# Block-sparse attention feeding soft mixture-of-experts slots: score groups, weight loads, slot steps and output halves in another order

## The chip, the cores and the metric

The kernel runs on one core of a Trainium2 chip. The metric is the device time of one execution in microseconds (us). Three executions were timed. A separate execution was recorded by the hardware profiler; all durations quoted from a profile belong to that one.

## The reference

q, k and v have the shape 4 x 8 x 768 x 64 (batch, head, position, width). First comes attention that keeps six chunks of 32 keys for each query:

```python
k_min, k_max = min/max of k over each chunk of 32 keys
ub = sum(maximum(q * k_min, q * k_max))        # an upper bound of the score, per query and chunk
top_chunks = argsort(where(causal, ub, -1e9))[..., -6:]
scores = where(sel & causal, q @ k.T / 8, -1e9)
x = softmax(scores) @ v                        # laid out as 3072 x 512
```

Its result goes through a soft mixture of 8 experts with 4 slots each:

```python
logits = x @ phi                               # 3072 x 32
d = softmax(logits over the 3072 rows)         # dispatch
slot_input = d.T @ x                           # 32 x 512
slot_out[e] = relu(slot_input[e] @ w1[e]) @ w2[e]      # 512 -> 1024 -> 512, per expert
out = softmax(logits over the 32 slots) @ slot_out     # combine, 3072 x 512
```

The inputs are float32 in HBM; the kernel loads them as bf16. Eight w1 and eight w2, each 2 MB in HBM and 1 MB as bf16, make 16 weights, called w_sb 0 to 15.

## The kernel before, in words

The work is cut into 16 pairs of heads; four pairs make a batch. A loop of steps, `for i in range(-2, NPAIR)` at L479, runs a software pipeline that is written out by hand: each engine runs its instructions in the order in which the step function calls stand there. In step i these pairs are at work:

- Pair i + 4: its k and q are loaded (`load`, L129). Pair i + 2: its v is loaded (`load_v`, L134); its k and q are transposed on TensorE and copied out by ScalarE (`transposes` L181, `evac_T` L190), and VectorE takes the chunks' minima and maxima (`kmin`, `kmax`) and splits q by sign (`qsplit`).
- Pair i + 1: upper bounds on TensorE (`ubound`), the six best chunks on VectorE (`select`: twelve MAX8 at L241 and a comparison at L244), and transposition of the selection (`ns_transposes`, `evac_ns`).
- Pair i: scores and exponentials. The 21 causal blocks of 128 x 128 are packed into six groups of 384 or 512 columns (table `GROUPS`). `scores(i, g)` makes one matmul for q and k (L270) and one or two for the mask (L280) for each piece of a group and head, into one of two PSUM buffers `sc`; `expo(i, g)` runs one exponential on ScalarE (L293) and masks the diagonal block on GpSimd (L295).
- Pair i - 1: product with v (`pv`, L314), in four portions. Pair i - 2: normalisation on VectorE (`normalise`, L326 and L327) and transposition of the result (`x_transposes`, `evac_x`).

When the last pair of a batch has come to step i - 3, the step is a slot step (steps 6, 10 and 14): the batch's logits get their running column maximum (`moe_max`: a transpose on TensorE; `moe_bound`: a maximum on VectorE, L379; `moe_exp`: broadcast matmul at L385 and subtraction on GpSimd; `moe_exp2`), the row maximum and exponentials of the combine weights (`moe_comb`, `moe_comb2`), the accumulation of the slot inputs (`moe_dispatch`, L439) and the transposed combine weights (`moe_ct`, L453 and L456). Logits are formed at the end of the step before (`moe_logits`). Small PSUM results share two rotating buffers `tp`.

All loads, the weights included, are issued on GpSimd's queue (L122, L129, L134), between that engine's masks and small operations. The table `wplan` (L468) says how many weights each step issues: weight 0 ahead of the loop, then one in step -1 and in each of the steps 2 to 15. Up to step 13 they are issued in the middle of the step, behind the v load; in steps 14 and 15, where space has come free, at the top.

Behind the loop comes the tail (from L568): the last pair's attention, the last batch's logits, maxima, dispatch and combine weights, with a few matmuls that do nothing but keep TensorE running (`keep`, L584). Then the experts: first layer (`experts_in`, L670; two halves f of the hidden width), transposition (`hidden_T`, L682), second layer (`experts_out`, L710; hidden half f, expert group g of four experts, output column half y), scaling by the slots' sums (`zsum`, L690; so_sb at L729 and L731) and the sums of the combine weights (`csums`, 24 matmuls at L697). Last, 24 row blocks of the output: two matmuls of 256 columns each (L749), a scaling by VectorE or ScalarE (L752 to L756) and a store on SP's queue (L759, L761), mostly of 512 KB.

Of the kernel before, what the change touches and what calls it, by code (L numbers as in the profile page):

```python
# [30 lines left out]
    [(0, 0, 384, 0)],  # L31
    [(1, 0, 256, 0), (0, 384, 128, 256)],
    [(2, 0, 512, 0)],
    [(5, 0, 128, 0), (1, 256, 384, 128)],
    [(3, 0, 384, 0)],
    [(4, 0, 256, 0), (0, 512, 256, 256)],
]
WIDTH = [sum(p[2] for p in g) for g in GROUPS]
BLOCK = {}
for _g, _pieces in enumerate(GROUPS):  # L40
    for _kg, _q0, _w, _c in _pieces:
        for _x in range(0, _w, P):
            BLOCK[(_kg, _kg + (_q0 + _x) // P)] = (_g, _c + _x)


@with_exitstack
def kernel(
# [41 lines left out]
    w_sb = []  # L89
    for i in range(EARLY):  # L90
        w_sb.append(static.tile([P, NDG * F], BF16, name=f"w_sb{i}"))
# [171 lines left out]
    def scores(i, g):  # L263
        ps = p_sc.tile([P, 2, 512], F32, name="sc_ps", tag="sc")
        kT, qT, nsT = st["kT", i], st["qT", i], st["nsT", i]
        for kg, q0, w, c in GROUPS[g]:
# [20 lines left out]
    def expo(i, g):  # L287
        w = WIDTH[g]
        if w == 512:
            e = ep.tile([P, 2, 512], BF16, name="e_sb", tag="e_sb")  # L290
        else:
            e = ep3.tile([P, 2, 384], BF16, name="e3_sb", tag="e3_sb")
        nc.scalar.activation(e[:, :, :w], st.pop(("scps", i, g))[:, :, :w], func=ACT.Exp, scale=scale)  # L293

        nc.gpsimd.affine_select(  # L295
            out=e[:, :, :P], in_=e[:, :, :P], compare_op=ALU.is_ge, fill=0.0,
            base=0, pattern=[[0, 2], [1, P]], channel_multiplier=-1,
        )
        st["e", i, g] = e

    def pv(i, ts):
# [7 lines left out]
        for t in ts:  # L309
            for h in range(2):  # L310
                o = at[:, h, (t - tb) * (D + 1):(t - tb + 1) * (D + 1)]
                for kg in range(t + 1):
                    g, c = BLOCK[(kg, t)]
# [68 lines left out]
    def moe_exp(b):  # L382
        lg = st["lg", b]
# [32 lines left out]
    def moe_comb(b):  # L416

        lg = st.pop(("lg", b))
# [31 lines left out]
    def moe_ct(b):  # L450
# [5 lines left out]
        nc.vector.tensor_copy(cT_all[:, b * NQT:(b + 1) * NQT, :], ps)  # L456
# [11 lines left out]
    wplan = {i: 1 for i in range(-1, NPAIR)}  # L468
    for i in (0, 1):
        wplan[i] = 0  # L470
# [8 lines left out]
    for i in range(-2, NPAIR):  # L479
# [4 lines left out]
        if have(i):  # L484
            scores(i, 0)
            expo(i, 0)
            scores(i, 1)
            expo(i, 1)
        moe(moe_max, i - 3)
        if have(i + 1):  # L490
            ubound(i + 1)
        if have(i - 2):
            normalise(i - 2)
        moe(moe_bound, i - 3)
        if have(i + 1):
            select(i + 1)
        if i == -1:
# [13 lines left out]
        moe(moe_exp, i - 3)  # L511
# [5 lines left out]
        moe(moe_exp2, i - 3)  # L517
# [4 lines left out]
        if have(i + 2):  # L522
            transposes(i + 2, "q")
            evac_T(i + 2, "q")
            kmin(i + 2)
        if have(i - 2):
# [4 lines left out]
        moe(moe_comb, i - 3)  # L531
# [4 lines left out]
        if have(i):  # L536
            scores(i, 4)
            expo(i, 4)
            if i == LAST:
                pv(i - 1, [5])  # L540
            scores(i, 5)
            expo(i, 5)
        moe(moe_comb2, i - 3)
# [68 lines left out]
    keep(2)  # L612
# [12 lines left out]
    nc.vector.tensor_reduce(rm, lg1, axis=AX.X, op=ALU.max)  # L625
    dm = small.tile([P, 1, NS], F32, name="dm", tag="dm")
# [13 lines left out]
    op = ctx.enter_context(tc.tile_pool(name="op", bufs=5))  # L640
# [17 lines left out]
    cinv = tail.tile([P, B * NQT], F32, name="cinv")  # L658
    zinv = tail.tile([P, 1], F32, name="zinv")
# [28 lines left out]
    def zsum():  # L688
        ps = p_tp.tile([P, 1], F32, name="z_ps", tag="tp")
        nc.tensor.matmul(  # L690
            ps, lhsT=zrow.rearrange("p j s -> p (j s)"), rhs=identf[:1, :1], start=True, stop=True)
        nc.vector.reciprocal(zinv, ps)

    def csums():
        ps = p_tp.tile([P, B * NQT], F32, name="cs_ps", tag="tp")
        for n in range(B * NQT):
            nc.tensor.matmul(  # L697
                ps[:, n:n + 1], lhsT=cT[:, n // 2, n % 2], rhs=ones_sq[:, :1], start=True, stop=True)
        nc.vector.reciprocal(cinv, ps)

    HD = Dm // 2
    so_t = p_at.tile([P, 2, 512], F32, name="so_ps", tag="at")
    so_ps = [so_t[:, y, :HD] for y in range(2)]
# [20 lines left out]
    experts_out(0, [0], [0, 1])  # L724
    hidden_T(1)
    zsum()
    experts_out(0, [1], [0, 1])
    experts_out(1, [0, 1], [0])
    nc.scalar.activation(so_sb[0], so_ps[0], func=ACT.Copy, scale=zinv)  # L729
    experts_out(1, [0, 1], [1])  # L730
    nc.scalar.activation(so_sb[1], so_ps[1], func=ACT.Copy, scale=zinv)  # L731
    csums()


    homes = ((p_sc, "sc"), (p_tp, "tp"), (p_sc, "sc"), (p_tp, "tp"), (p_at, "at"))
    n = 0
    for m in range(B * NQT // 2):
        o_sb = op.tile([P, 2, Dm], F32, name="o_sb", tag="o_sb")
        rows = out[m * 2 * P:(m + 1) * 2 * P, :].rearrange("(p x) d -> p x d", x=2)
        for x in range(2):  # L740
            pool, tag = homes[n % 5]
            if n == 0:
                o_ps = pool.tile([P, 2, Dm], F32, name="o2_ps", tag=tag)
                halves = [o_ps[:, y, :HD] for y in range(2)]
            else:
                o_ps = pool.tile([P, Dm], F32, name="o_ps", tag=tag)
                halves = [o_ps[:, y * HD:(y + 1) * HD] for y in range(2)]
            for y in range(2):
                nc.tensor.matmul(halves[y], lhsT=cT[:, m, x], rhs=so_sb[y], start=True, stop=True)  # L749
            if n == 0:  # L750
                for y in range(2):
                    nc.vector.tensor_scalar_mul(o_sb[:, x, y * HD:(y + 1) * HD], halves[y], cinv[:, n:n + 1])  # L752
            elif x == 0:
                nc.vector.tensor_scalar_mul(o_sb[:, x, :], o_ps, cinv[:, n:n + 1])
            else:
                nc.scalar.activation(o_sb[:, x, :], o_ps, func=ACT.Copy, scale=cinv[:, n:n + 1])  # L756
# [35 lines left out]
```

## Time and profile before

| what | value |
|---|---|
| timed executions | 172.8, 171.62, 171.58 us; median 171.62 |
| the profiled execution | 172.21 us, its span 170.5 us |
| PE (TensorE matmul) busy | 137.8 us, 81% of the span, 2574 instructions |
| PEld (TensorE weight load) busy | 99.3 us, 58% |
| DVE (VectorE) busy | 121.5 us, 71% |
| ACT (ScalarE) busy | 122.6 us, 72% |
| POOL (GpSimd) busy | 104.0 us, 61% |
| HBM read / written | 52.49 MB / 6.29 MB |
| chain of work that ended last | PE 39%, ACT 21%, DVE 15%, DMA 14%, issue 5% |
| weight loads | 16 of 1024.0 KB, 14.4 us from issue to landing (median) |
| mean granted TensorE clock | 0.98 |

Times in the profile are counted from the start of the span. In lines of a timeline the first column is the start, the second the duration of one instruction or of a run of equal ones (xcount), then engine, line and operation with the tiles written and read; in brackets stands how long the engine had been idle, and what ended that. The line of slices cuts the span into 40 equal parts; a digit is the busy share in tenths. A DMA's time to landing runs from its issue on the queue to the arrival of its last byte.

### The profile page before, as it was taken

What the parts mean: (1) busy time and instruction counts of PE and PEld (TensorE: products, weight loads), DVE (VectorE), ACT (ScalarE), POOL (GpSimd) and SP (SyncE); (2) the same over time, 40 slices, a digit from 0 to 9 for tenths busy, and PEclk for the clock granted to TensorE, in tenths of its full rate; (3) what the DMA queues carried; (4) which work ended last, traced back from release to release, by engine and by line L of the source; (5) the groups of instructions that cost most, each with busy time, mean ns of one, the idle gap of its engine ahead of it and who ended that gap; (6) DMA issues with size and microseconds to landing.
All of it is one profiled execution on the core that took longest, in us unless ns stands there. A gap on an engine that the chain in (4) does not pass through costs nothing.

```text
span 170.5 us, 6183 instructions
## 1 busy us (share of the span) xinstructions
PE 137.8 (81%) x2574; PEld 99.3 (58%) x2575; DVE 121.5 (71%) x416; ACT 122.6 (72%) x166; POOL 104.0 (61%) x202
## 2 busy tenths in 40 slices
PE   0458988999999898999999899979889989896300
PEld 0335555777666767766776667657566855763200
DVE  3468768999999976999997798988742651166510
ACT  3355999999999877999987799978777522175510
POOL 7977759788878777888878878547663800000000
PEclk9999999999999999999999999999999999999965
DMA  3999999999999999999999999999999980029995
GB/s 46 163 156 185 182 212 188 129 152 184 184 214 190 211 197 209 193 211 195 212 197 205 196 207 202 203 203 200 202 208 212 215 163 13 4 76 407 404 400 195
DMA packets 40460, 32.94 MB, mean 193 GB/s; under 512 B 26352, under 2 KB 34544, under 8 KB 40432
## 3 DMA queue, kind: packets, MB, share of 16 engines
q0 software_dynamic: 38416, 26.25, 104.2%
q1 hardware_dynamic: 2016, 6.29, 9.4%
q8 instruction: 20, 0.33, 0.7%
q14 instruction: 8, 0.07, 0.1%
HBM read 52.49 MB, written 6.29 MB: 345 GB/s over the span
## 4 chain that ended last, share of the span: by engine, by line
PE 39%; ACT 21%; DVE 15%; DMA 14%; issue 5%; POOL 2%; DVEq 0%; ACTq 0%; POOLq 0%
ACT e_sb L293 15%; DMA k_in<-in_k_dram 10%; PE sc_ps L270 7%; PE at_ps L314 5%; PE tr_ps L181 5%; PE sc_ps L280 5%; DMA out_dram<-o_sb 4%; DVE x_sb L327 3%; PE h_ps L670 2%; PE so_ps L710 2%; DVE qpn L216 2%; PE ub_ps L229 2%; DVE mx L241 2%; ACT qT L190 2%; PE xT_ps L336 2%
## 5 line engine op out<-in xcount | busy, mean ns | idle before, releaser
L293 ACT ACTIVATE e_sb<-sc_ps 128x768 bf16<-128x768 f32 (+1 forms) x96 | 82.9, 930 | 9.7 <-PE sc_ps L280 9.7
L295 POOL TENSOR_SCALAR_AFFINE_SELECT e_sb<-e_sb 128x256 bf16<-128x256 bf16 x96 | 38.7, 413 | 19.6 <-ACT e_sb L293 18.9
L270 PE MATMUL sc_ps<-qT,kT 64*128 64x384 bf16 (+3 forms) x288 | 40.3, 299 | 4.2 <-ACT e_sb L293 4.1
L280 PE MATMUL sc_ps<-nsT,smask 64*128 64x384 bf16 (+2 forms) x320 | 38.6, 281 | 0.0
L314 PE MATMUL at_ps<-v_t,e_sb 128*128 128x65 bf16 x672 | 29.8, 194 | 1.5 <-DVE x_sb L327 1.2
L314 PEld LDWEIGHTS <-e_sb 128*128 128x128 bf16 x672 | 25.3, 98 | 3.9 <-DVE x_sb L327 1.2
L270 PEld LDWEIGHTS <-kT 64*128 64x128 bf16 x288 | 17.0, 95 | 15.5 <-issue 10.4
L241 DVE MAX8 mx<-ub_ps 128x8 f32<-128x8 f32 (+1 forms) x192 | 16.9, 161 | 3.6 <-PE ub_ps L229 2.0
L280 PEld LDWEIGHTS <-smask 64*128 64x128 bf16 x320 | 16.6, 96 | 3.8 <-issue 0.6
L199 DVE TENSOR_REDUCE mm<-kT 128x24 bf16<-128x768 bf16 x16 | 15.1, 945 | 4.6 <-ACT kT L190 4.5
L190 ACT COPY kT<-tr_ps 128x768 bf16<-128x768 bf16 x16 | 12.8, 799 | 7.5 <-PE tr_ps L181 6.7
L134 POOL DMA_DIRECT2D v_t<-in_v_dram x16 | 16.7, 1045 | 2.0 <-PE ns_ps L252 1.4
L327 DVE TENSOR_TENSOR x_sb<-at_ps,inv 128x768 bf16<-128x768 f32 (+1 forms) x17 | 15.5, 911 | 0.6
L205 DVE TENSOR_REDUCE mm<-kT 128x24 bf16<-128x768 bf16 x16 | 15.1, 943 | 0.0
L181 PE MATMUL tr_ps<-ident,k_in 128*64 128x128 bf16 x192 | 9.4, 240 | 6.3 <-DMA k_in<-in_k_dram 5.5
L190 ACT COPY qT<-tr_ps 128x768 bf16<-128x768 bf16 x16 | 12.9, 805 | 2.0 <-PE tr_ps L181 2.0
L129 POOL DMA_DIRECT2D k_in<-in_k_dram x16 | 11.7, 729 | 1.5 <-POOLq L776 0.8
L122 POOL DMA_DIRECT2D w_sb<-in_moe_w_dram x16 | 11.4, 710 | 1.5 <-DMA w_sb<-in_moe_w_dram 1.5
L756 ACT ACTIVATE o_sb<-o_ps,cinv 128x512 f32<-128x512 f32 x12 | 8.1, 686 | 4.9 <-PE o_ps L749 2.4
L129 POOL DMA_DIRECT2D q_in<-in_q_dram x16 | 11.5, 720 | 0.0
L216 DVE TENSOR_SCALAR qpn<-qT 128x768 bf16<-128x768 bf16 x16 | 11.0, 685 | 0.0
L347 DVE COPY xT_sb<-xT_ps 128x768 bf16<-128x768 bf16 (+1 forms) x15 | 8.1, 540 | 4.0 <-PE xT_ps L336 3.9
(116 smaller groups left out, 196.5 us busy)
## 6 DMA issues: line engine op xcount, KB each, us to landing
w_sb<-in_moe_w_dram POOLq DMA_DIRECT2D x16, 1024.0 KB, 14.4
out_dram<-o_sb SPq DMA_DIRECT2D x10, 512.0 KB, 4.9
k_in<-in_k_dram POOLq DMA_DIRECT2D x16, 192.0 KB, 9.7
q_in<-in_q_dram POOLq DMA_DIRECT2D x16, 192.0 KB, 10.0
v_t<-in_v_dram POOLq DMA_DIRECT2D x16, 192.0 KB, 10.8
out_dram<-o_sb SPq DMA_DIRECT2D x4, 256.0 KB, 3.4
phi_sb<-in_moe_phi_dram POOLq DMA_DIRECT2D x1, 32.0 KB, 9.0
```

The costliest lines, as they stand in the source:

```text
L129: nc.gpsimd.dma_start(out=t, in_=src.rearrange("h (p g) d -> p h (g d)", p=P))
L134: nc.gpsimd.dma_start(out=v_t[i % NV][:, :, :, :D], in_=v[b, 2 * j:2 * j + 2].rearrange("h (g p) d -> p h g d", p=P),)
L181: nc.tensor.matmul(ps[h * 64:(h + 1) * 64, g, :], lhsT=src[:, h, g * D:(g + 1) * D], rhs=ident, is_transpose=True,)
L190: nc.scalar.copy(t.rearrange("d (p g) -> d p g", g=NQT), st.pop((nm + "ps", i)).rearrange("d g p -> d p g"),)
L199: nc.vector.tensor_reduce(mm[:, 0, 0, :], kT, axis=AX.X, op=ALU.min)
L241: nc.vector.max(mx[:, a, :], ub[:, a, :max(8, 4 * t + 4)])
L270: nc.tensor.matmul(ps[:, h, c:c + w], lhsT=kT[r, kg * P:(kg + 1) * P], rhs=qT[r, qs], start=True, stop=False,)
L280: nc.tensor.matmul(ps[:, h, c + (f - t0) * P:c + (l - t0) * P], lhsT=smask[r, x, kg].rearrange("p a b -> p (a b)"), rhs=nsT[r, (f - x * NJ ...
L293: nc.scalar.activation(e[:, :, :w], st.pop(("scps", i, g))[:, :, :w], func=ACT.Exp, scale=scale)
L295: nc.gpsimd.affine_select(out=e[:, :, :P], in_=e[:, :, :P], compare_op=ALU.is_ge, fill=0.0, base=0, pattern=[[0, 2], [1, P]], channel_mult ...
L314: nc.tensor.matmul(o, lhsT=st["e", i, g][:, h, c:c + P], rhs=v_t[i % NV][:, h, kg, :], start=(kg == 0), stop=(kg == t),)
L327: nc.vector.tensor_tensor(st["x", b][:, t0:t1, 2 * j:2 * j + 2, :].rearrange("p t h d -> p h t d"), at[:, :, :, :D], inv.broadcast_to([P, ...
```

## The change

Six edits come together.

1. The score groups are packed and ordered anew: both groups that open a step are 512 columns wide, the next two 384. A step makes 16 score matmuls and 18 mask matmuls instead of 18 and 20; the widths are three times 512 and three times 384 as before. Group 4 now holds two diagonal blocks and group 5 none. The last pair has a table of its own.
2. `wplan`: weight 0 stays ahead of the loop, then one weight in each of the steps 2, 4, 5, 6, 8, 9, 10 and 12, two in step 13, three at the top of step 14 and two at the top of step 15.
3. In a slot step the column maximum's transpose stands between the scores of groups 0 and 1, its maximum ahead of normalisation; the row maxima follow selection; the exponentials and the remaining slot operations move to other places. The copy of the last but one batch's transposed combine weights is put off into step 15.
4. In the tail the sums of the combine weights of the first three batches are made where two `keep` matmuls stood, those of the last batch with the slots' sums; the reciprocals follow them.
5. The second expert layer is reordered: column half 0 for all eight experts comes first. The halves have PSUM buffers of their own.
6. The first three pairs of row blocks of the output are made and stored by column halves (1 KB a row): those of half 0 before and during the second layer's last part for half 1, those of half 1 behind it. The w1 weights lie in a pool of their own that is closed behind the first layer, and the output buffers take its place.

```diff
 GROUPS = [
-    [(0, 0, 384, 0)],
-    [(1, 0, 256, 0), (0, 384, 128, 256)],
     [(2, 0, 512, 0)],
     [(5, 0, 128, 0), (1, 256, 384, 128)],
+    [(0, 0, 384, 0)],
     [(3, 0, 384, 0)],
-    [(4, 0, 256, 0), (0, 512, 256, 256)],
+    [(4, 0, 256, 0), (1, 0, 256, 256)],
+    [(0, 384, 384, 0)],
 ]
+GROUPS_LAST = [
...
-            out=e[:, :, :P], in_=e[:, :, :P], compare_op=ALU.is_ge, fill=0.0,
-            base=0, pattern=[[0, 2], [1, P]], channel_multiplier=-1,
-        )
+        for kg, q0, _, c in pieces:
+            if q0 == 0:
+                nc.gpsimd.affine_select(
+                    out=e[:, :, c:c + P], in_=e[:, :, c:c + P], compare_op=ALU.is_ge, fill=0.0,
...
-        nc.vector.tensor_copy(cT_all[:, b * NQT:(b + 1) * NQT, :], ps)
+        st["ctps", b] = ps
+        if b != B - 2:
+            moe_ct_copy(b)
...
-    wplan = {i: 1 for i in range(-1, NPAIR)}
-    for i in (0, 1):
-        wplan[i] = 0
+    wplan = {i: 1 for i in (2, 4, 5, 6, 8, 9, 10, 12)}
+    wplan.update({13: 2, 14: 3, 15: 2})
...
             scores(i, 0)
             expo(i, 0)
+        moe(moe_max, i - 3)
+        if have(i):
             scores(i, 1)
             expo(i, 1)
-        moe(moe_max, i - 3)
         if have(i + 1):
             ubound(i + 1)
+        moe(moe_bound, i - 3)
         if have(i - 2):
             normalise(i - 2)
-        moe(moe_bound, i - 3)
+        if i == LAST:
+            moe_ct_copy(B - 2)
         if have(i + 1):
             select(i + 1)
+        moe(moe_comb, i - 3)
...
             pv(i - 1, [0, 1, 2])
-        moe(moe_exp, i - 3)
         if have(i):
             scores(i, 2)
             expo(i, 2)
             scores(i, 3)
             expo(i, 3)
-        moe(moe_exp2, i - 3)
+        moe(moe_exp, i - 3)
...
             kmin(i + 2)
+        moe(moe_exp2, i - 3)
...
         moe(moe_scale, i - 3)
-        moe(moe_comb, i - 3)
...
+        moe(moe_comb2, i - 3)
+        if have(i):
             scores(i, 5)
             expo(i, 5)
-        moe(moe_comb2, i - 3)
...
-    keep(2)
+    csa = p_tp.tile([P, BL * NQT], F32, name="cs_ps", tag="tp")
+    for b in range(BL):
+        col_sums(csa[:, b * NQT:(b + 1) * NQT], b)
...
-    experts_out(0, [0], [0, 1])
+    w_ctx.close()
+    op = ctx.enter_context(tc.tile_pool(name="op", bufs=5))
+    experts_out(0, [0, 1], [0])
     hidden_T(1)
-    zsum()
-    experts_out(0, [1], [0, 1])
+    sums()
+    experts_out(0, [0], [1])
     experts_out(1, [0, 1], [0])
     nc.scalar.activation(so_sb[0], so_ps[0], func=ACT.Copy, scale=zinv)
+    experts_out(0, [1], [1])
+    half_out(0, 0)
+    half_out(1, 0)
     experts_out(1, [0, 1], [1])
     nc.scalar.activation(so_sb[1], so_ps[1], func=ACT.Copy, scale=zinv)
-    csums()
+    half_out(2, 0)
+    for m in range(NH):
+        half_out(m, 1)
...
```

A half is made and stored by this function, and `experts_out` stands at L743 of the changed kernel:

```python
    def half_out(m, y):
        o_sb = op.tile([P, 2, HD], F32, name="oh_sb", tag="oh_sb", bufs=2 * NH)
        for x in range(2):
            tag = next(half_homes[y])
            o_ps = homes[tag].tile([P, HD], F32, name="oh_ps", tag=tag)
            nc.tensor.matmul(o_ps, lhsT=cT[:, m, x], rhs=so_sb[y], start=True, stop=True)
            scaled(x, o_sb[:, x, :], o_ps, 2 * m + x)
            if m == y == 0:
                nc.sync.dma_start(out=rows(m)[:, x, :HD], in_=o_sb[:, x, :])
        if m + y > 0:
            nc.sync.dma_start(out=rows(m)[:, :, y * HD:(y + 1) * HD], in_=o_sb)
```

## The prediction

> **What bounds the kernel now.** I read the slices of the page first, then the table of busy time by stretches, then the timelines of GpSimd (which issues every load), of ScalarE and of the tail, and last the times to landing of single loads.
>
> ```profile
> DMA  3999999999999999999999999999999980029995
> GB/s 46 163 156 185 182 212 188 129 152 184 184 214 190 211 197 209 193 211 195 212 197 205 196 207 202 203 203 200 202 208 212 215 163 13 4 76 407 404 400 195
> ```
>
> A slice is 4.26 us. The DMA engines are busy from the second slice to slice 33 (141 us), rest while the experts run, and are busy again with the output. The loads write bf16 and read float32, so 205 GB/s here is 410 GB/s read.
>
> ```profile
> 29.40:36.25 6.85, 6.54 (x126) 4.73 (x126) 6.46 (x23) 6.51 (x9) 5.49 (x11) 1.00 1.27 144
> 57.40:66.50 9.10, 7.73 (x159) 5.89 (x157) 6.87 (x26) 7.25 (x12) 6.67 (x13) 1.00 1.30 202
> 128.00:137.00 9.00, 8.36 (x180) 6.54 (x182) 4.04 (x10) 5.53 (x7) 5.07 (x9) 1.00 1.07 214
> 153.00:163.00 10.00, 4.56 (x30) 2.80 (x29) 6.38 (x9) 5.86 (x9) 0.00 (x0) 1.00 1.02 404
> 163.00:164.00 1.00, 0.00 (x0) 0.00 (x0) 0.14 (x1) 0.05 (x1) 0.00 (x0) 0.79 1.04 410
> 164.00:168.00 4.00, 0.00 (x0) 0.00 (x0) 0.00 (x0) 0.00 (x0) 0.00 (x0) 0.50 1.00 394
> ```
>
> Columns: PE, PEld, DVE, ACT, POOL busy, granted clock, DMA share, GB/s. An ordinary step (first row) has PE, DVE and ACT each at 6.5 of 6.85 us. A slot step (second row) leaves PE idle for 1.4 us. Third row: with only weights in flight, 214 GB/s at a share of 1.07: 1.049 MB takes 4.9 us, and that is the DMA engines' full rate, as the output's 404 (fourth row) confirms from the other side. The clock falls to half about 2.2 us after the last matmul (161.3).
>
> ```profile
> 116.80 1.03 POOL L134 DMA_DIRECT2D v_t<-in_v_dram  x1
> 117.83 0.70 POOL L122 DMA_DIRECT2D w_sb<-in_moe_w_dram  x1
> 119.29 0.72 POOL L122 DMA_DIRECT2D w_sb<-in_moe_w_dram  x1
> 125.95 0.77 POOL L122 DMA_DIRECT2D w_sb<-in_moe_w_dram  x1
> ```
>
> ```profile
> DMA to landing us min/median/max: 10.7/10.7/10.7
> DMA to landing us min/median/max: 17.0/17.0/17.0
> DMA to landing us min/median/max: 10.2/10.2/10.2
> ```
>
> These are: the last v load (116.80, so it lands at 127.5), the last weight (125.95, lands at 143.0), and a weight issued into a nearly empty queue (35.49). Loads land in the order of issue. The last v and the three weights behind it took 127.5 to 143.0: a backlog is being worked off. The second expert layer begins at 144.4 and needs every weight, so the last one arrives only 1.4 us early. That margin is the number to watch.
>
> ```profile
> 41.35 3.22 ACT L293 ACTIVATE e_sb<-sc_ps 128x768 bf16<-128x768 f32 x4
> 44.69 0.80 ACT L190 COPY kT<-tr_ps 128x768 bf16<-128x768 bf16 x1
> 45.71 1.94 ACT L293 ACTIVATE e_sb<-sc_ps 128x1024 bf16<-128x1024 f32 x2 [0.22 <-PE sc_ps L280]
> 146.05 1.93 PE L710 MATMUL so_ps<-w_sb,hT_pad 128*32 128x256 bf16 x64
> 148.03 0.47 ACT L729 ACTIVATE so_sb<-so_ps,zinv 128x256 bf16<-128x256 f32 x1 [2.79 <-PE so_ps L710]
> 151.73 0.84 SPq L759 DMA_DIRECT2D out_dram<-o_sb  x2
> 4.85 0.85 PE L181 MATMUL tr_ps<-ident,k_in 128*64 128x128 bf16 x12 [4.85 <-DMA k_in<-in_k_dram]
> 44.12 0.53 PE L181 MATMUL tr_ps<-ident,k_in 128*64 128x128 bf16 x12
> ```
>
> ScalarE's gaps in an ordinary step are 0.12 and 0.22 us. The tail's stages follow. The last two rows are the same twelve transposes before PE had worked and in mid loop: 0.85 against 0.53 us.
>
> The profiled execution took 172.21 us, 1.71 more than its span of 170.5, and 0.59 more than the median of 171.62.
>
> **The change, part by part.** First the loop, as far as it moves the issue of the last loads.
>
> Wide groups first: ScalarE has 1.94 us of exponentials instead of 1.5 before the copy of kT, which covers PE's 1.24 us of bounds, transposes and values, so both gaps (0.34 us) can go. PE runs 4 short matmuls fewer; 384 columns in one piece take 0.35 us (47.18 to 47.53), in two 0.43 (43.16 to 43.59), so 0.08 us, hidden while ScalarE sets the pace. With three engines at 6.5 us I take 0.22 a step, between 0 and 0.34. Nine ordinary steps come before the last v load: 2.0 (0 to 3.1). The masks stay six a step on GpSimd (two for group 4, none for group 5).
>
> Slot steps: PE's three waits were 0.39 (for the maximum behind normalisation), 0.41 and 0.56 us. The first goes, the other two shrink as their producers run earlier; new is that the maximum's transpose, now ahead of group 1, can wait some 0.3 us for the reduction on VectorE (done at 57.24; group 0's scores end at about 57.1), with group 1's scores queued behind it, and that normalisation and selection start 0.5 us later on VectorE. I take 1.3 a slot, between -0.3 and 1.6; two slots: 2.6.
>
> The k load that ScalarE waited 0.87 us for at 113.28 (normally 0.12) took 12.8 us to land behind the backlog. With fewer weights ahead of it this goes: 0.75.
>
> Sum 5.35 us: the last v load is issued at 116.80 - 5.35 = 111.45 (109.4 to 117).
>
> Late weights: before, fourteen weights are issued up to the middle of step 13 and one at the top of steps 14 and 15. Now it is eleven, then three and two. By step 12 four weights fewer have been loaded, and steps -1, 3, 7 and 11 have none, so the queue runs dry there: k, q and v take 3.5 us (landings of one step: a weight at 111.7, then 112.7, 113.7, 115.2) of a 6.6 us step. That capacity is lost, and the weights are moved to where nothing else hides them. Weight 8 is issued alone, one step before: 111.45 - 6.65 + 1.03 = 105.8. It lands 10.2 later, at 116.0; v 1.5 later, 117.5; then seven weights at 4.9: 34.3, so the last lands at 151.8. Bounds: 2.9 less, if the lone weight holds nothing up (10.2 against 2.4 of latency and 4.9 of transfer), 1.0 more, since the last two landed 5.4 apart. On GpSimd's queue the issues cost 0.70 us each: one more in step 13, two more at the top of 14, one more at 15, ahead of masks; the idle rows there (1.90, 0.51, 0.29) cover most, at most 1.4 shows, and it shows before the wait that swallows it.
>
> The Trainium skill's page "DMA: Bandwidth & Descriptors", section "Bandwidth", gives HBM about 358 GB/s a core. The third row reads 428 (2 x 214), so this trace disagrees.
>
> The tail: the first group of the second layer for half 0 now takes all eight experts before anything else, so PE stands at expert 7's first matmul until 151.8. All that stands ahead (end of the loop, column sums in place of two idle matmuls, first layer) ends at about 139 and is hidden; if that cover went, 18 column sums cost 0.45 us (24 took 0.6 at L697) against 0.43 for the two removed. Behind the landing: 13 + 16 + 32 matmuls at 27 ns (64 from 146.05 to 147.75), 1.65, and 0.27 to come out; four transposes 0.35; z and six column sums 0.46; so_sb 0.48; half an output matmul 0.32, its scaling 0.48, and issue, 0.2. Sum 4.2. PE has then waited in pieces of 4.9 us, so by the 2.2 us above its clock is at half. Two rows price that: 0.85/0.53 = 1.6, and 0.61 for a 384-column score group at 13.34 against 0.35, 1.74. PE's 3.0 us grow by 2.2 (0 if the clock holds, 3.0 at twice the time). All of it stays slow: at the start PE worked almost without pause from 13.3, and a 384-wide score pair still took 0.50 at 19.77.
>
> The Trainium skill's page "TensorE: Matmul & The Clock Gate", Part 1, has the clock at half after an idle window of about 3.4 us and back after as long a busy one, a rule that speaks against this change. By it the extra would be half of 3.4, 1.7 us, and the forecast 178.0; this trace's slow 6.5 us at the start say longer.
>
> The output: before, first store to end of span took 170.5 - 151.73 = 18.8, at 404 GB/s throughout. Same bytes now. A quarter goes in 1 KB pieces: rows on both sides are k (1.5 KB pieces, 393 KB read in 0.97, 405 GB/s) and v (256 B, 1.5 us, 262 GB/s), so 0 to 2.1 us more; nearer to k, with a short gap before half 1: 0.5. Three stores more on SP's queue hide under transfers of 0.65 us each.
>
> Sum: 151.8 + 4.2 + 2.2 + 18.8 + 0.5 = 177.5 span; with 1.7 around it 179.2; less 0.6 to stand beside the median, 178.6. **I forecast 178.5 us, slower by 4%.**
>
> **The rivals.** (a) Weights as late, but PE keeps its clock: 176.3. For it: a few matmuls run at each landing. Against: 2.2 us sufficed at the end.
> (b) The other side: the last weights land in time, because the loads overlap more than I reckon. Then the loop's gain of 6.65 (three slots) and of the tail's new order count: from 144.4 the first store takes 4.8 instead of 7.3. 172.2 - 6.65 - 2.5 + 0.5 - 0.6 = 163.0. It decides if the last weight lands by 138.5. From the v's landing at 117.5 that leaves 21 us for seven weights that take 34 at the third row's rate.
> (c) No measurable change: last landing before 146.5, or 148.5 with the clock kept: 171.7 to 173.3. It needs the loop's largest gain and the lone weight to hold nothing up.
> (d) The reordering gains nothing, its new waits eating it: everything 5.4 later, 184.
> (e) Weights slower when seven stand in a row, 5.9 us each, as between the landings at 132.2 and 138.1, instead of 4.9: 185. Against it: the next took 4.9 (143.0). The Trainium skill's 358 GB/s, from the page named above, would also give 5.9.
>
> **How the numbers follow.** Forecast 0.64, (a) 0.12, (b) 0.08, (c) 0.06, (d) 0.07, (e) 0.03. Within 1% is about what a measurement of this kernel can't tell from no change: 169.9 to 173.3. Slower: 0.64 + 0.12 + 0.07 + 0.03 = 0.86; same 0.06; faster 0.08. The forecast's own spread (landing 149 to 154, clock 1.8 to 3.0) is 175.5 to 181.5. Range: 172.5 to 182.5, taking in (a) and most of (c), leaving out (b), (d), (e).
>
> **What would show it.** Right: slices of 40 to 100 us with GB/s well under 200; last weight issued at about 120 and landing near 152; PE idle in waits ended by weights between 138 and 152, before L743; granted clock of 0.5 there; first store near 158, then 400 GB/s to the end. Loop: ScalarE's 0.12 and 0.22 gone, slot steps 1.3 shorter. Wrong: PE enters the second layer without a wait on a weight, or the last weight lands before 147.

## The result, and the profile after

| kernel | median us | range | against before, 95% interval |
|---|---|---|---|
| before | 171.83 | 171.58 to 172.8 | |
| after | 181.51 | 179.67 to 182.32 | 1.054 [1.045, 1.063] |

The changed kernel is slower by 5.4%. Its profiled execution took 181.71 us, with a span of 179.8; the one before took 172.21 with 170.5. (Ratios leave out executions more than 1.5% above the fastest of their kernel, medians keep them; of the profiles quoted below only that of the changed kernel with the table of before belongs to such an execution.)

The slices of the page come first. A slice is now 4.5 us. PEclk is the granted clock, GB/s what the DMA engines moved.

```profile
PEclk9999999999999999999987999999999955589755
GB/s 52 164 169 176 189 76 125 119 200 179 121 197 186 215 191 209 174 164 198 184 206 196 199 55 169 177 206 213 213 217 215 210 217 136 4 65 357 405 403 171
```

Four holes stand out: 76 (slice 6, at 22 to 27 us), 125 and 119 next to it, 121 (slice 11), and 55 (slice 24, at 103 to 108 us). They lie where the steps -1, 3 and 11, which now issue no weight, leave the queue dry. In stretches: 136 GB/s between 20 and 40 us (172 before), 187 between 40 and 100 (202), 132 between 100 and 112 (199), 186 between 112 and 120 (204). Times their lengths the differences are 0.72 + 0.90 + 0.80 + 0.14 = 2.6 MB, or 12 us at 214 GB/s. Of these, 1.1 us come back between 120 and 140 us (216 against 204). The last weight lands 10.1 us later than before (153.05 against 142.99).

The PE timeline shows who pays for it. Each line: start, duration, the instruction, and in brackets how long PE had been idle and for what.

```profile
140.90 0.71 PE L743 MATMUL so_ps<-w_sb,hT_pad 128*32 128x256 bf16 x17
143.29 0.27 PE L743 MATMUL so_ps<-w_sb,hT_pad 128*32 128x256 bf16 x1 [1.69 <-DMA w_sb<-in_moe_w_dram]
148.19 0.37 PE L743 MATMUL so_ps<-w_sb,hT_pad 128*32 128x256 bf16 x1 [4.63 <-DMA w_sb<-in_moe_w_dram]
153.09 1.01 PE L743 MATMUL so_ps<-w_sb,hT_pad 128*32 128x256 bf16 x13 [4.53 <-DMA w_sb<-in_moe_w_dram]
...
155.34 3.34 PE L743 MATMUL so_ps<-w_sb,hT_pad 128*32 128x256 bf16 x64
```

PE enters the second layer at 140.90, 3.5 us earlier than before (144.42), and then stands for the weights of experts 5, 6 and 7 for 10.8 us in all, one single matmul or so between the waits. The last line is the same 64 matmuls that took 1.93 us before. The table by stretches says why they now take 3.34:

```profile
141.00:153.00 12.00, 1.25 (x23) 0.51 (x14) 0.00 (x0) 0.60 (x1) 0.00 (x0) 0.65 0.91 182
153.00:159.50 6.50, 6.41 (x105) 4.58 (x108) 1.02 (x5) 0.89 (x3) 0.00 (x0) 0.59 0.01 3
```

The column ahead of the last two is the granted clock: 0.65 in the wait, 0.59 behind it. The first store is issued at 159.54 (151.73 before). From there to the end of the span it is 20.3 us (18.8 before).

```profile
159.54 0.85 SPq L778 DMA_DIRECT2D out_dram<-oh_sb  x2
```

The loop is faster, though not where the prediction had it. An ordinary step takes 6.50 us (6.87 before), and ScalarE runs through it without a gap (no brackets stand behind the copy of kT and the exponentials that follow):

```profile
42.98 0.81 ACT L206 COPY kT<-tr_ps 128x768 bf16<-128x768 bf16 x1
43.82 1.51 ACT L310 ACTIVATE e_sb<-sc_ps 128x768 bf16<-128x768 f32 x2
```

The slot steps, measured from a step's first exponential to the next step's, are not shorter: 9.40, 9.77 and 8.51 us (steps 6, 10 and 14) against 9.46, 9.58 and 7.75. ScalarE and GpSimd in step 6 show what came in:

```profile
61.54 0.36 ACT L425 ACTIVATE d_sb<-ld 128x192 bf16<-128x192 f32 x1 [1.43 <-POOL ld L413]
```

```profile
58.24 0.51 POOL L441 TENSOR_TENSOR lc<-lg,rm 128x192 f32<-128x192 f32 x1 [0.54 <-DVE rm L439]
58.70 0.74 POOL L145 DMA_DIRECT2D k_in<-in_k_dram  x1
59.44 0.72 POOL L145 DMA_DIRECT2D q_in<-in_q_dram  x1
60.16 0.78 POOL L314 TENSOR_SCALAR_AFFINE_SELECT e_sb<-e_sb 128x256 bf16<-128x256 bf16 x2
60.91 0.60 POOL L413 TENSOR_TENSOR ld<-lg,m_run 128x192 f32<-128x192 f32 x1
```

The five lines are GpSimd's queue in its order. `rm` are the row maxima, `lc` the logits less the row maxima, `ld` the logits less the running column maximum. The row maxima, moved ahead, put `lc`, and a wait of 0.54 us for them, in front of the k and q issues and two masks, and only behind these comes `ld`, for which ScalarE stands 1.43 us. In step 14 the two further weight issues add to it: 8.51 us here, 8.15 in a kernel that differs in the table of weights alone and issues one weight there (`wplan[14] = 1`, below).

### The profile page after: what moved, and what is told of

Its sections match the earlier page's. It is cut to its first block, busy times and chain, and to the rows that moved or that the text cites. A ratio compares the mean times of both kernels' runs of the same rounds, so it can differ in the third digit from the quotient of the medians.

```text
span 179.8 us, 6069 instructions
## 1 busy us (share of the span) xinstructions
PE 140.7 (78%) x2516; PEld 98.0 (54%) x2517; DVE 120.6 (67%) x418; ACT 122.6 (68%) x169; POOL 104.0 (58%) x202
## 4 chain that ended last, share of the span: by engine, by line
PE 27%; ACT 24%; DMA 21%; POOL 9%; DVE 9%; issue 6%; SPq 0%; DVEq 0%; POOLq 0%; ACTq 0%
DMA w_sb<-in_moe_w_dram 16%; ACT e_sb L310 14%; PE sc_ps L286 5%; PE sc_ps L296 4%; PE tr_ps L197 4%; ACT qT L206 3%; POOL e_sb L314 3%; PE at_ps L333 3%; PE so_ps L743 3%; ACT kT L206 3%; DMA out_dram<-o_sb 3%; POOL w_sb L138 2%; DMA k_in<-in_k_dram 2%; PE ub_ps L245 2%; DVE mx L257 2%
## 5 line engine op out<-in xcount | busy, mean ns | idle before, releaser
L310 ACT ACTIVATE e_sb<-sc_ps 128x1024 bf16<-128x1024 f32 (+1 forms) x96 | 83.2, 919 | 3.9 <-PE sc_ps L296 3.6
L314 POOL TENSOR_SCALAR_AFFINE_SELECT e_sb<-e_sb 128x256 bf16<-128x256 bf16 x96 | 39.0, 422 | 21.2 <-ACT e_sb L310 20.9
L286 PE MATMUL sc_ps<-qT,kT 64*128 64x384 bf16 (+3 forms) x258 | 38.0, 315 | 2.4 <-ACT e_sb L310 1.5
L296 PE MATMUL sc_ps<-nsT,smask 64*128 64x384 bf16 (+2 forms) x294 | 39.7, 295 | 0.0
L286 PEld LDWEIGHTS <-kT 64*128 64x128 bf16 x258 | 14.2, 95 | 10.5 <-issue 5.3
L150 POOL DMA_DIRECT2D v_t<-in_v_dram x16 | 17.2, 1075 | 1.1 <-PE ns_ps L268 0.8
L296 PEld LDWEIGHTS <-smask 64*128 64x128 bf16 x294 | 15.3, 97 | 3.9 <-issue 0.8
L743 PE MATMUL so_ps<-w_sb,hT_pad 128*32 128x256 bf16 x128 | 6.8, 350 | 10.8 <-DMA w_sb<-in_moe_w_dram 10.8
L789 ACT ACTIVATE so_sb<-so_ps,inv_b 128x256 bf16<-128x256 f32 x1 | 0.5, 474 | 16.4 <-PE so_ps L743 16.4
L743 PEld LDWEIGHTS <-hT_pad 128*32 128x32 bf16 x128 | 4.3, 122 | 12.8 <-issue 11.8
```

The source lines that it names most:

```text
L150: nc.gpsimd.dma_start(out=v_t[i % NV][:, :, :, :D], in_=v[b, 2 * j:2 * j + 2].rearrange("h (g p) d -> p h g d", p=P),)
L286: nc.tensor.matmul(ps[:, h, c:c + w], lhsT=kT[r, kg * P:(kg + 1) * P], rhs=qT[r, qs], start=True, stop=False,)
L296: nc.tensor.matmul(ps[:, h, c + (f - t0) * P:c + (l - t0) * P], lhsT=smask[r, x, kg].rearrange("p a b -> p (a b)"), rhs=nsT[r, (f - x * NJ ...
L314: nc.gpsimd.affine_select(out=e[:, :, c:c + P], in_=e[:, :, c:c + P], compare_op=ALU.is_ge, fill=0.0, base=0, pattern=[[0, 2], [1, P]], ch ...
L743: nc.tensor.matmul(so_ps[y][j * CH:(j + 1) * CH, :], lhsT=hT_pad[:, fg, e, :], rhs=w_sb[E + e][:, fg * Dm + y * HD:fg * Dm + (y + 1) * HD] ...
```

## The experiments

Two theories stood against each other at first. The first: weights issued late come late, because the queue ran dry earlier; everything else in the change is worth something. The second: the new order of slots and output costs the time. Later ones took apart the clock, the slot steps, the groups and the output. All ratios are against the kernel before on the same chip; the last four kernels (the groups, the tail with idle matmuls, the two of the output's start) ran on another chip than the other experiments, and there the kernel before took 171.53 us against 171.57 to 171.84.

**The weights: the table of before in the changed kernel, and the changed table alone.**

```diff
-    wplan = {i: 1 for i in (2, 4, 5, 6, 8, 9, 10, 12)}
-    wplan.update({13: 2, 14: 3, 15: 2})
+    wplan = {i: 1 for i in range(-1, NPAIR)}
+    for i in (0, 1):
+        wplan[i] = 0
```

> The changed kernel with the table of weight loads of the kernel before (one weight in step -1 and in each of the steps 2 to 15); all else stays changed. Theory (late weights are the cause, everything else together is a gain): the last v load is issued at 112 to 114, the last weight lands at 139 to 143 instead of 153.05, PE's waits on weights ahead of the second layer shrink from 10.8 us to 2 or less, first store at 145 to 148, time 166 to 169 us. Rival 1 (the new output order or the reordered slot steps cost the time): the last weight lands 10 us earlier and the time stays above 178. Rival 2 (the DMA engines are full anyway, so the plan only shifts which load is late): the k, q and v loads land late, PE and ScalarE wait on them in the loop, and the time is between 170 and 178.

Measured: median 170.62 us of ten executions that spread from 167.96 to 171.65; the ratio, 0.983 [0.978, 0.988], stands for 168.9. Undoing the table alone takes 11 to 13 us back, and rival 1 is out. By the ratio the time lies in the theory's range, by the median of all ten in that of rival 2. The profiled execution is the slowest of the ten, so its waits need not be those of the others. In it the last weight lands at 139.8, no weight is waited for, the second layer begins at 144.64 and the first store is issued at 149.45, later than the theory had it. One PE line names the place:

```profile
110.61 0.63 PE L197 MATMUL tr_ps<-ident,k_in 128*64 128x128 bf16 x12 [2.24 <-DMA k_in<-in_k_dram]
```

This k was issued at 96.61 and landed at 110.57, 14 us later, behind a backlog of weights. The clock is then at half for 3.4 us (from 110.9), and step 13 takes 10.9 us in place of 7.1.

The mirror image, the kernel before with the changed table:

> The kernel before with nothing but the changed table of weight loads. Theory (late weights are the cause): without the loop's gain the last v load is issued near 116, the last weight lands at 154 to 157, PE waits on weights for 8 to 12 us ahead of the second layer, time 182 to 186 us, slower than the changed kernel by 1 to 4 us. Rival 1 (the weights alone do little): within 2 us of 171.8.

Measured: 184.14 us, 1.070 [1.063, 1.077], within the range of the theory. The last weight lands at 155.94.

```profile
155.98 3.57 PE L709 MATMUL so_ps<-w_sb,hT_pad 128*32 128x256 bf16 x61 [4.52 <-DMA w_sb<-in_moe_w_dram]
```

Three waits of 9.6 us in all, and slow matmuls behind them, without any other part of the change. The table alone costs 12.3 us (184.14 - 171.84); all other parts together bring 2.6 with it (184.14 - 181.51) and, without it, 2.9 by the ratio of 0.983 or 1.2 by the median of all ten.

**Weights still earlier.** One weight in each of the steps -1 to 11, then in 14 and 15.

> The changed kernel with one weight in each of the steps -1 to 11 and one in steps 14 and 15, so that the loads stand earlier than in either kernel. Theory (the DMA engines' capacity in mid loop is what counts, and idle capacity there is free): the last weight lands at 136 to 140, no wait on weights ahead of the second layer, first store at 145, time 164 to 167 us, at or below the changed kernel with the table of before. Rival (the weights ahead of k, q and v make those late): waits of PE on k and q loads appear in the steps 2 to 12, the second layer begins after 142, and the time is 168 us or more.

Measured: 178.98 us, 1.037 [1.028, 1.046]. The theory fell. What the rival named is there (PE waits on k seven times in the loop, 8.0 us together; the second layer begins at 152.31), and its "168 us or more" left the size open. Something comes in that neither named: GpSimd itself stands still, ten times and for 18.8 us (total, times, longest):

```profile
POOL w_sb L138 <- DMA w_sb<-in_moe_w_dram: 18.8, 10, 3.8
```

The weight issued at 61.01 waits for the landing, at 60.72, of the weight issued eight loads earlier. So do those at 69.12 (68.83), 77.24 (76.95) and 85.36 (85.08). In the trace the 65 loads use eight semaphores by turns, and there are never more than eight under way; when the ninth waits, the masks behind it on GpSimd's queue wait with it. The kernel before meets the same limit three times, for 1.5 us together. How the loss divides between this and the waits on k was not tried.

**The clock.** The changed kernel with idle matmuls in the waits:

```diff
+                    for _ in range({5: 7, 6: 20, 7: 20}.get(e, 0) if f == y == fg == 0 else 0):
+                        nc.tensor.matmul(
+                            h_ps[1][:, 1, :], lhsT=ident, rhs=w_sb[E][:, :512], start=True, stop=True)
```

> The changed kernel with 7, 20 and 20 matmuls of 512 columns that do no useful work, put ahead of the first second-layer matmul of experts 5, 6 and 7, so that PE works while it would wait for a weight. Theory (the clock at half costs 2.2 us behind the last landing): the last weight lands at 153 as before, the granted clock stands at 1.0 from the landing on, the 64 matmuls that took 3.34 us take about 1.9, the first store is issued 4.2 to 4.7 us behind the landing instead of 6.5, time 179 to 179.6, 2 to 2.5 us less than the changed kernel. Rival (the 6.5 us are waits among engines and not the clock): clock at 1.0, and the time within 0.7 us of the changed kernel.

Measured: 180.57 us (179.32 to 181.46), 1.049 [1.041, 1.056], 0.9 less than the changed kernel by the medians and 2.4 by the profiled executions. The median misses the theory's 179 to 179.6 and the intervals overlap, so the times alone settle nothing. The stage does:

```profile
147.93 4.49 PE L744 MATMUL h_ps<-w_sb,ident 128*128 128x512 bf16 x20
...
154.04 1.93 PE L746 MATMUL so_ps<-w_sb,hT_pad 128*32 128x256 bf16 x64
```

The 64 matmuls take 1.93 us again. From the last landing (152.58) to the first store (156.98) it is 4.40 us, against 6.49 (153.05 to 159.54) without the idle matmuls. The clock's price behind the landing is 2.1 us.

**One weight from step 7 to step 13**, all else as in the changed kernel with the table of before:

```diff
+    wplan = {i: 1 for i in (-1, 2, 3, 4, 5, 6, 8, 9, 10, 11, 12, 13, 14, 15)}
+    wplan[13] = 2
```

> The changed kernel with the table of weight loads of the kernel before, but the weight of step 7 moved to step 13 (so one in the steps -1, 2 to 6 and 8 to 12, two in 13, one in 14 and in 15). Theory (two limits: the DMA engines must never run dry, and no weight may stand so far ahead that k comes late): the queue is never empty, so the last weight lands at 139 to 141 as with the table of before; the wait of 2.24 us on the k load near 108 is gone, because one weight (4.9 us) less stands ahead of it; the second layer begins at 141, first store at 145.5 to 146.5, time 167 to 168.5 us. Rival 1 (the k wait has another cause than the backlog): the wait stays and the time is 169 to 171. Rival 2 (any weight moved back comes late): PE waits on the last weight for 2 us or more, time above 170.

Measured: 167.11 us, 0.973 [0.969, 0.977]. The theory holds in its numbers: of the waits on k one of 0.8 us is left (beside that at the start), the last weight lands at 140.38, the second layer begins at 141.47, the first store is issued at 146.28. The interval lies clear of the 0.983 [0.978, 0.988] with the table of before. The same change that made the kernel 5% slower makes it 2.7% faster with another table.

**The slot steps**, on top of this table. First with the row maxima behind the column maximum's subtraction, so that `ld` stands ahead of `lc`:

```diff
-        moe(moe_comb, i - 3)
...
         moe(moe_exp, i - 3)
+        moe(moe_comb, i - 3)
```

> The kernel with the weight of step 7 moved to step 13, and in the slot steps the row maxima (and their subtraction on GpSimd) put behind the column maximum's subtraction instead of behind selection, so that on GpSimd's queue ld stands ahead of lc. Theory (ld is late because lc and the k and q issues stand ahead of it on GpSimd): ScalarE's wait for ld of 1.4 us a slot step shrinks to 0.9 or less, slot steps are 0.3 to 1.0 us shorter, time 0.5 to 2.5 us less than with lc first. Rival (ld waits for the broadcast maximum, not for GpSimd's queue): the wait stays at 1.2 us or more, and the time is within 0.5 us.

Measured: 166.56 us, 0.970 [0.968, 0.973]; 0.55 less by the medians, with intervals that overlap: no difference in time is shown. The mechanism is plain in the trace. ScalarE and GpSimd in step 6:

```profile
60.38 0.36 ACT L425 ACTIVATE d_sb<-ld 128x192 bf16<-128x192 f32 x1 [0.41 <-POOL ld L413]
```

```profile
59.75 0.59 POOL L413 TENSOR_TENSOR ld<-lg,m_run 128x192 f32<-128x192 f32 x1
60.31 0.50 POOL L441 TENSOR_TENSOR lc<-lg,rm 128x192 f32<-128x192 f32 x1
```

The wait shrinks from 1.44 to 0.41 us, and the slot steps from 9.41, 9.52 and 8.15 us to 8.38, 8.53 and 8.14. The second layer begins at 139.02, 2.4 us earlier. A part of this is lost at once, because now a weight is late again, and 1.7 us arrive at the first store (144.58 against 146.28) and at the end of the span. The medians differ by less; the profile with `lc` first is of the longest of that kernel's four executions (168.57; the others 166.53 to 167.68).

```profile
140.22 0.60 PE L743 MATMUL so_ps<-w_sb,hT_pad 128*32 128x256 bf16 x13 [0.48 <-DMA w_sb<-in_moe_w_dram]
```

Then with the slot steps in the order of the kernel before:

> The kernel with the weight of step 7 moved to step 13, and the slot steps in the order of the kernel before (column maximum behind group 1 and behind normalisation, row maxima behind the slot scaling). Groups, tail and output stay changed. Theory (the new slot order only exchanged waits, 9.46 us a slot step before and 9.40 after): within 0.7 us of the kernel with the new slot order. Rival (the new order is worth the 1.3 us a slot step of the prediction): 2.5 to 4 us slower than with the new order.

Measured: 166.43 us, 0.969 [0.966, 0.972]. The theory holds: 0.7 us less than with the new order, and the intervals overlap. The three slot steps take 9.19, 9.31 and 7.32 us, 25.8 together, against 27.1 in the new order as it was made and 25.1 with `ld` first. No difference in time between the slot orders is shown; the 2.5 to 4 us of the rival are out.

**The groups.** The kernel with `ld` first and the score groups of before:

> The kernel with the weight of step 7 moved to step 13 and ld ahead of lc, but with the score groups of the kernel before in every step (384 columns first). Theory (the wide groups are worth 0.35 us in each of 12 or 13 ordinary steps, and that reaches the end): the last v load is issued 3.5 to 4.5 us later, the second layer begins at 142 to 144 instead of 139.0, time 168.5 to 171 us. Rival (the DMA engines set the end: the last weight lands at 140.2 whatever the loop does): the last weight lands at 140 to 141, the second layer begins by 141, time below 168.

Measured: 169.76 us, 0.988 [0.982, 0.995], 3.2 us slower. Theory: ordinary steps are back at 6.87 us, the last v load is issued 4.3 us later (114.20 against 109.93), and the first exponential of step 15 comes 4.5 us later (124.96 against 120.47). The rival has its part too: of 4.5 us in the loop 2.8 are left at the start of the second layer (141.81 against 139.02), while in this profile the clock holds in the tail (below) where it dips in the other; and the weight that lands at 141.63 is not waited for. At the first store 2.0 us are left (146.62 against 144.58). The other 1.2 of the 3.2 us come in the output, which takes 21.5 us here and 20.3 there, with the same instructions: the fourth store is issued 1.9 us behind the third.

**The tail alone**, in the kernel before (the changed second layer, sums and output halves):

> The kernel before with the changed tail, second layer and output halves alone; groups, weight loads and slot steps stay as before. Theory (from the second layer's start to the end 25.2 us instead of 26.1, since the first store comes 2.5 us earlier and the 1 KB pieces take back 1.5): 170.3 to 171.5 us, 0.4 to 1.4 less than before. Rival 1 (the whole 2.5 us less 0.5 of the prediction): 169.2 to 170. Rival 2 (all that stands ahead has become later, or a weight is waited for): 171.8 or more.

Measured: 172.78 us, 1.005 [1.002, 1.009]. The theory fell: from the second layer's start to the end of the span it is 26.2 us and not 25.2. Rival 2 holds as well: the second layer begins at 145.42, a full microsecond later than before, although the loop ends no later. The first layer begins so:

```profile
139.45 1.90 PE L685 MATMUL h_ps<-w_sb,siT_pad 128*32 128x512 bf16 x16 [0.37 <-DVE siT_pad L662]
```

Sixteen matmuls take 1.90 us that took 1.05 before. The granted clock is at half from 139.34 to 142.75. Two idle matmuls of 512 columns stood where this kernel has the column sums (at 136.58). They turn out to have had a purpose. Put back, with the sums of one column each behind the dispatch:

> The kernel before with the changed tail, second layer and output halves alone, but with the two idle matmuls of 512 columns back in their place, and the column sums of the first three batches behind the dispatch. Theory (the column sums, one column wide, do not hold the clock as the two idle matmuls did, so the first layer ran at half clock): granted clock 1.0 through the first layer, its first 16 matmuls take 1.05 us instead of 1.90, the second layer begins 0.7 to 1.2 us earlier than the 145.42 without them, and the time is 0.7 to 1.3 us less than without them, at or just below the kernel before. Rival (the clock falls there for another reason): 1.90 again, within 0.3 us.

```profile
137.10 0.59 PE L588 MATMUL h_ps<-w_sb,ident 128*128 128x512 bf16 x2
...
139.97 1.05 PE L685 MATMUL h_ps<-w_sb,siT_pad 128*32 128x512 bf16 x16
```

Measured: 171.61 us, 0.998 [0.995, 1.001], 1.2 us less than without them, as the theory said: 1.05 us again and the second layer at 144.45. Over the profiles of this study, one for each kernel: with the two idle matmuls the first layer is at full clock in 3 of 3 kernels, without them it runs its first sixteen matmuls at half in 7 of 11, the changed kernel not among the 7. It seems to be a matter of the execution and not of the kernel: of the ten executions of the tail alone, four took 171.2 to 171.9 us at a mean clock of 0.963 to 0.968, five, the profiled one among them, 172.6 to 173.7 at 0.956 to 0.959, and one 177.4 at 0.939. A half-clock stretch of 3.4 us lowers the mean over 171 us by 0.010. With the idle matmuls all twelve stand at 0.963 to 0.971.

This kernel also tells what the halves do. Its first store is issued at 149.27, 2.46 us ahead of the kernel before (151.73), and its span ends at the same 170.5. All of it is given back in the output (21.2 us against 18.7).

```profile
149.27 1.75 SPq L753 DMA_DIRECT2D out_dram<-oh_sb  x2
151.12 3.28 SPq L755 DMA_DIRECT2D out_dram<-oh_sb  x5
```

SP issues a half store every 0.65 to 0.7 us, just as long as 256 KB take at 400 GB/s, so nothing piles up behind the first; and here the third is issued 1.4 us after the second (149.70 and 151.12).

**The output's start.** Two more runs, on top of `ld` first: the half stores of the second pair issued by GpSimd, and no halves at all.

```diff
+            q = nc.gpsimd if m == 1 else nc.sync
+            q.dma_start(out=rows(m)[:, :, y * HD:(y + 1) * HD], in_=o_sb)
```

> The kernel with the weight of step 7 moved to step 13 and ld ahead of lc; of the half stores, those of the second pair of row blocks are issued by GpSimd instead of SP. Theory (the output's start is slow because SP issues a store of 256 KB only every 0.65 to 0.7 us, which is as long as its transfer): first store to end of span 0.4 to 1.0 us shorter than 20.3, time 165.5 to 166.2. Rival (the 1 KB pieces themselves are slow, or the halves are not ready earlier): within 0.3 us of 166.56.

Measured: 168.45 us, 0.977 [0.969, 0.984]. The theory fell. From the first store (144.23) to the end (165.2) it is 21.0 us, 0.7 more than with one queue.

```diff
-    NM, NH = B * NQT // 2, 3
+    NM, NH = B * NQT // 2, 0
```

> The kernel with the weight of step 7 moved to step 13 and ld ahead of lc, the second layer in its new order, but all row blocks of the output made and stored in full width (2 KB a row) as before. Theory (the halves bring the first store forward by 2.3 us and give back 1.5): first store near 147, 18.8 us from there to the end of the span, time 167.0 to 168.0. Rival (the halves give back all that they gain): within 0.3 us of 166.56.

Measured: 167.31 us, 0.971 [0.963, 0.978]. The first store comes at 147.38 and the output takes 18.8 us, both as expected; but in this profile the clock is at half from 141.57 to 144.99, in the second layer, and 96 matmuls take 4.47 us there that take 2.99 (1.93 + 1.06) elsewhere. Without these 1.5 us the halves' lead would be 1.3 us, or 1.8 counted from the landing of the last weight (139.74 here, 140.18 with halves): about the 1.5 that they give back. The intervals overlap with those of the kernel with halves: no difference is shown.

The best kernels of the study are those with the weight moved from step 7 to 13 and either `ld` first or the old slot order: 3% faster than before.

## Why the prediction was right, and where it missed

The direction, the cause and the place were right: the table of weights alone costs 12.3 us, the wait is on the weights of the last experts, and the clock behind it is at half. Of the sum, against a measured 181.51 us:

- *Last v load issued at 111.45.* Measured 112.76, a gain of 4.0 us and not 5.35. An ordinary step gains 0.36, not 0.22: both of ScalarE's gaps went entirely. The k load's 0.75 came as said (step 13: 8.43 to 7.12 us, an ordinary gain included). The step that failed is the slot steps' 1.3 each: they gain 0.06, lose 0.19 and lose 0.76. The text priced PE's three waits and a delay on VectorE. It did not follow the row maxima onto GpSimd's queue, where `lc` now stands ahead of two DMA issues (1.46 us) and two masks (0.78 us), and `ld` behind them all. Taking that out again made two slot steps 1.0 us shorter. That the loop misses by 1.3 us only is partly luck: two slots short of 1.3 each (2.7 us together) and the dip below are made up in part by the ordinary steps and by 0.6 us up to the end of step 0 (21.71 against 22.35) that the sum did not have.
- A clock dip was not foreseen: half clock from 93.42 to 96.83, in slot step 10 and the next. The kernel with idle matmuls, whose loop is the same instruction for instruction, shows none. By the lengths of these two steps in it (9.52 and 6.66; here 9.77 and 7.42) the dip costs 1.0 us.
- *Seven weights at 4.9 us, last landing at 151.8.* From the last v issue to the last landing: 40.35 predicted, 40.29 measured. The landing came at 153.05 because the v load came 1.3 late. Rival (e), 5.9 us a weight, is out.
- *Landing to first store 4.2 + 2.2.* Measured 6.49, of which 2.1 are the clock by the run with idle matmuls. Rival (a) is out: the few matmuls at each landing did not hold the clock; seven, twenty and twenty idle ones ahead of them did. That all 3.0 us of PE would stay slow came nearly true: the clock came back at 158.27, 5.2 us behind the landing and 1.3 ahead of the first store.
- *Output 18.8 + 0.5.* Measured 20.3. The term that was mis-sized is the halves' price, 1.5 and not 0.5 (its bounds were 0 and 2.1). Why some half stores stand 1 us further apart than others (in four of the kernels with halves, whose output takes 20.6 to 21.5 us instead of 20.3) stays open; a second queue did not help.
- The rest of the 3.0 us between forecast and median: 1.3 (loop) + 1.0 (output) + 0.2 (1.9 instead of 1.7 around the span) + 0.4 (the profiled execution is 0.2 above its median, not 0.6) = 2.9.

The signs it named: last weight issued at 123.73 ("about 120"); waits ended by weights before L743; clock 0.59 behind them; ScalarE's gaps gone. Wrong: "slices of 40 to 100 us well under 200" are at 187 in the mean (202 before); the holes lie more at 20 to 40 and 100 to 112. And slot steps 1.3 shorter.

Rival (b), weights in time, 163.0, was tried by another table: it comes to 166.4 to 167.1. Of the difference, the landing is 140.2 where (b) asked for 138.5, and the halves take 1.5 and not 0.5. An estimate from the measured rates puts a floor under the landing: sixteen weights at 4.9 and sixteen times k, q and v at 3.5 us are 134.4 us of DMA time, and the first k lands at 4.8. In every kernel with the table of before, or with one weight of it moved, the last weight lands between 139.7 and 143. Rival (d), the reordering gains nothing, is half true: true of the slots, not of the groups, which brought 3.2 us to the end, 2.0 of them up to the first store.

The Trainium skill's page "TensorE: Matmul & The Clock Gate", Part 1, describes a free-running window of 3413 ns. The traces agree: each half-clock stretch in the middle of an execution lasts one window or four (93.42 to 96.83; 144.62 to 158.27), and the changes of one execution lie a whole number of windows apart. By its rule the clock was to come back after one busy window, and the prediction worked out 1.7 us from it; since the window does not start with the work, the first whole window behind the landing at 153.05 ran from 154.86 to 158.27, the stretch was 5.2 us long, and the price 2.1.

## What to carry to other kernels

A load that is moved to a later place costs nothing only if the queue never runs dry in between: add up what the queue carries (bytes over the measured rate) and look for the slices that fall below it, since that capacity does not come back. Moving it too early has a price as well, by what lands behind it and by the number of loads that may be under way; of the four tables tried here the best was that of before with one weight moved from step 7 to step 13. And of an instruction that is moved, follow every product onto the queue of the engine that makes it: a reduction on VectorE moved forward held up GpSimd, and through it ScalarE and PE.

## What the runs showed of the hardware that was not expected

- PE can be occupied and still lose the clock. In the 3.4 us ahead of the fall in the first layer PE was occupied for 84 to 94% of the time (7 kernels), mostly by narrow matmuls of 1 to 192 columns. With two idle ones of 512 columns more the clock stayed at 1.0 (3 of 3 kernels). The fall cost 0.85 us in the first sixteen matmuls alone.
- A count that tells the two cases apart, worked out from the traces and not tried by a run of its own: cut the fourteen profiles into the windows of 3.413 us at whose ends the clock changes, and sum, over the matmuls that start in a window, the moving columns times the share of the 128 x 128 array that the matmul uses. 28 windows at full clock were followed by half clock. 26 of them hold at most 2374 such columns, the other two 2560 and 3020 (this one is the dip in slot step 10). The 537 others at full clock hold at least 2434. The experts' matmuls use 32 of 128 columns of the array and so count a quarter.
- Waits of PE on a load, of 1.76, 1.82, 1.97 and 2.24 us, with matmuls on either side, were each followed by half clock for 3.4 us; the next longest in the loop, 1.31 and 1.34 us, were not.
- Loads that cast float32 to bf16 ran at 214 GB/s written, 428 read, with weights alone, and at most 217 in a slice of the page after; k, q and v together reach 168 (0.59 MB in 3.5 us).
